# A gated mix of a state-space layer and linear attention on one Trainium2 core: the last fold of K's weight moved ahead of the vectors' transposes, eight idle products removed, the first two x tiles swapped, the last two rows scaled in halves

## The chip, the core and the metric

The kernel runs on one core of a Trainium2 chip. The metric is the time of one execution in device microseconds. The engines are named as in the profile: PE is TensorE (PEld its weight loads), DVE is VectorE, ACT is ScalarE, POOL is GpSimd, and SP is SyncE, which here only issues transfers. Each engine works through its own list of instructions in order and waits on semaphores of the others.

## What is computed

The input x has 2048 rows of 512 columns. Two branches take it, and a gate mixes them row by row.

```python
g = sigmoid((x * gate_w).sum(-1, keepdims=True))
# A: a diagonal complex recurrence
Lam_bar = exp(exp(log_dt) * Lam);  B_bar = ((Lam_bar - 1) / Lam)[:, None] * Bmat
h_t = Lam_bar * h_{t-1} + B_bar @ x_t
a = 2 * (hseq @ Cmat.T).real + x * Dskip
# B: linear attention, 32 heads of 16
q, k, v = split(x @ wqkv)
phi(u) = concat(softmax(u @ w_phi), softmax(-(u @ w_phi)))
kv = phi(k)^T v;  z = sum phi(k);  o = phi(q) kv / (phi(q) z + 1e-6)
out = g * a + (1 - g) * (o @ wo)
```

All inputs and the output are bfloat16.

## The kernel before, in words

The work is cut into stages, and each stage is a Python generator that yields after every few instructions. A string, `ORDER`, names a stage per word, and the loop at L804 takes one step of that stage for each word. So the string is the order in which instructions are issued, for all engines together; each engine gets its own instructions in that order. After a word, `@` gives the PSUM banks that the step takes, `:D` sends a copy out of PSUM to VectorE instead of ScalarE, `:A` sends a store to ScalarE's queue instead of SyncE's, and `F:n` issues n idle products (L810 to L812) of a constant tile into a bank that nothing reads. The loads of the first x tiles, of the weight of V (`Wv`) and of the small vectors stand ahead of that loop: SyncE issues the transposing loads of x tiles 0 to 3, then `Wv`, then tiles 4 to 7.

The words that the change and the prediction's steps touch:

- `W0` to `W3` (`st_W`, L271): TensorE transposes one block of K's weight, and a copy brings it back.
- `f0` to `f3` (`st_f`, `fold`, L428): four products of 128 columns multiply a block of K's weight by `w_phi`, and a copy writes the block of the folded weight `Wk2`.
- `V` (`st_V`, L308): TensorE transposes the three small vectors of the recurrence, VectorE copies them. `P`, `P2`, `P3`, `P4` and `U` compute the recurrence's angles and sizes from them, `i0` to `i3` tables of sines.
- `k0` to `k15` and `v0` to `v15` (L477, L484): four products of 512 columns for one tile of 128 rows of x, and one copy out of the bank. A product `k` needs its x tile and the four blocks of `Wk2` in turn.
- `l8` to `l15`: the loads of the later x tiles on SyncE.
- `o12` to `o15` (`st_o`, L725): the attention output of one tile of rows. For these four, TensorE transposes the result (L753) and the second-to-last step copies it out of PSUM (L755) into `oT`.
- `t0` to `t15` (`st_t`, L761): first step, four products of `oT` with `Wo` into the bank `py`; second step, the bank scaled by the gate `G` into the tile `ot`; third step, the store to the output. Row tiles are numbered in the order in which they are worked on, so t14 and t15 are the last two of 16.

The string ends, before and after the change, with these words:

```
t10:D t11 o15@2 o15 t10 o13:D t11 t11:A y13 t13 o14
o14@1 t15 t15 t15 o14:D t14 t13 t13 t14 t14:A
```

That is: row 14's transposes, then t15's products, t15's scaling, t15's store, the copy of row 14's `oT` on VectorE, t14's products, the scaling and store of t13, the scaling and store of t14.

Of the kernel before, what the change touches and what calls it, by code (L numbers as in the profile page):

```python
# [10 lines left out]
ALU = mybir.AluOpType  # L11
# [9 lines left out]
P = 128  # L21
MAGIC = 12582912.0
Z_MAX = 70.0
ORDER = """
NR F:28 NI B W1@0 W0@1 W0 W2@2 W1:D W3@3 W3 f1@4 W2:D f0@5 f2@6 f0 f1:D l10 V@0 F:4 V P f3@1 f3 f2:D F:4 P P k1@2 k1
l13 P2 k0@3 P2 U P2 P2 P2 P2 P4 k2@4 P3 P3 k3@5 P4 P4 k0 v0@0 i0 i2 U i0 i0 i1 i2 k4@7 i0:D i0 k2 i2 i2:D i2 U k3 k5@6
i1 v3@1 n0 x0 l9 i1 V2@2 i3 l12 x0 k4 v2@3 i3 i3 l14 i1 k5 n0 x0 n0 x0 i3 k7@4 n0 x0 U n0 i1 l11 k6@5 n1 x1 x1 n1 x1
n1 l8 R0 R1 x1 i3 k7 M v7@7 x1 n1 n1 k6:D L V2 v1@6 x2 n2 e0 v6@4 v5@5 v4@2 e0 x2 s0 v0 l15 n2 s0 n2 v2 s0 v1 R2 s0 v6
v3 n2 k10@0 k10 s0 k9@3 k9 C4 k13@6 gw D R3 s0 k12@4 e1 v7 s0 e1 s1 C6 k11@1 k11 x2 s1 k14@0 k8@3 k12 k14 k8 v4 k13
a0@71 a0 x2 s1 x2 s1 v5 g00@4 g00 g60@0 n2 x3 s1 g20@3 g60 s1 g10@2 g10 n3 e2 g30@6 g40@5 g10 s1 a1 x3 g20 n3 a1 x3 n3  # L30
x3 g41@4 n3 C3 e2 e2 e2 x3 g30 g40 g30 k15@0 k15 n3 e3 s2 x4 s2 x4 g01@2 g01 e3 e3 s2 g50@3 g11@5 g50 s2 s2 s2 n4 x4
n4 Q3 n4 s2 g50 g21@6 e3 s3 v8@0 g31@2 g11 Q2 g11 n4 g70@3 Q1 s3 C7 g21 g70 v9@5 g70 g70 z0 z0 g31 g31 Q0 w1@6 C0 a2
a2 a2 w0@3 s3 z0 v11@2 v9 g61@5 g41 R4 z0 w1 v8 z0 z0 g61 s3 w2@4 s3 s3 a2 x4 z0 z0 g51@6 g51 x4 w2 C2 s3 w3@0 g51 v11
n4 R5 w3 g71@5 g71 g71 g71 z1 z1 g02@4 g02 g42@6 a3 a3 z0 z0 g42 w0 e4 e4 z1 z1 z1 g62@2 g12@0 q1@5 C1 h50@4 C5 J1 e4
e4 z1 q2@6 q2 g12 g12 g22@3 g22 J0 h50 z1 z1 g62 q3@4 q3 J2 s4 z1 s4 q0@6 z1 s4 q0 q1 xA nA g32@0 J3 g32 g32 h60@3 J0
g52@2 g52 c4 h60 J2 c4 g52 h51@4 c2 s4 s4 g72@6 R7 g72 xA h10@5 nA g72 g72 c2 xA J3 nA h10 v10@0 v10 J1 s4 c5 h51 c5
R6 g23@3 v12@2 c4 c0 c0 g63@5 nA z2 z2 a3 a3 g03@4 xA g03 z2 z2 z2 z2 xA g23 z2 z2 g33@6 c5 v12 z2 z2 g13@0 g13 g63
g43@4 h32@3 g13 nA g43 h52@2 h52 g33 h32 h61@5 h61 h12@0 c0 g53@4 h12 g33 g53 s4 v14@3 c2 eA eA h42@2 h42 g73@6 g53 eA
# [30 lines left out]
def kernel(  # L69
# [18 lines left out]
    nc = tc.nc  # L88
    _, S, D = A_x.shape
# [5 lines left out]
    NTI = S // P  # L95
    NR = 8
# [7 lines left out]
    x2 = A_x[0]  # L104
# [3 lines left out]
    VS = nc.vector.tensor_scalar  # L108
# [3 lines left out]
    sel = {"banks": [], "eng": "act"}  # L112
# [66 lines left out]
    G = const.tile([P, NTI], F32, name="G")  # L179
# [581 lines left out]
    def st_t(n):  # L761
        ti = order[n]
        py, oT = live["py", n], live["oT", n]
        for g in range(HG):
            MM(out=py[:], lhsT=oT[:, g, :], rhs=Wo[:, g, :], start=False, stop=(g == HG - 1))  # L765
        yield
        ot = pools["op"][1].tile([P, D], BF16, name="ot", bufs=14)
        if sel["eng"] == "act":
            nc.scalar.mul(out=ot[:], in_=py[:], mul=G[:, ti:ti + 1])  # L769
        else:  # L770
            VS(out=ot[:], in0=py[:], scalar1=G[:, ti:ti + 1], scalar2=None, op0=ALU.mult)
        yield
        sel["q"].dma_start(out=out_par[:, ti // 2, ti % 2, :], in_=ot[:])
        yield
# [17 lines left out]
    for n in range(NTI):  # L792
        st.update({f"k{n}": st_k(n), f"v{n}": st_v(n), f"q{n}": st_q(n), f"y{n}": st_y(n), f"o{n}": st_o(n), f"t{n}": st_t(n)})
# [10 lines left out]
    for tok in ORDER.split():  # L804
        tok, _, eng = tok.partition(":")
# [42 lines left out]
```

## Time and profile before

| what | value |
|---|---|
| median of 3 runs | 155.96 us (155.78, 155.96, 157.13) |
| the profiled execution | 155.28 us |
| its span, first to last instruction | 153.2 us, mean granted TensorE clock 0.995 |
| TensorE busy | 146.2 us (95% of the span) |
| VectorE busy | 132.4 us (86%) |
| ScalarE busy | 129.2 us (84%) |
| transfers | 17.55 MB, 115 GB/s on the mean |

How to read the lines below. A row of the timeline gives the start (us from the span's start), the duration in us from the first start to the last end, engine, line, operation, output <- input, shapes and the number of merged instructions; a bracket at the end gives the idle time of that engine just before, and what ended it. Products are pipelined: one of 512 columns is shown with 0.38 us, while the next follows 0.22 us later. A row of the groups by shape ends with busy us, mean ns of one, idle us before them and what ended it. In the chain of waits each piece stands with its start, its duration and what it was. A row of the windows gives the stretch, its length, the busy time and count of each engine, then the granted TensorE clock (1.00 is full), the busy share of the DMA engines and GB/s. A few records of products are missing from the trace.

### The profile page before, as it was taken

The numbers are of one execution on the slowest core, as the hardware profiler recorded it, in microseconds if no ns is written. First come the engines' busy times: TensorE is split into PE (matmuls) and PEld (weight loads), VectorE is DVE, ScalarE is ACT, GpSimd is POOL, SyncE is SP. The second block draws the span as 40 slices with busy tenths as digits, with TensorE's granted clock in tenths as the row PEclk, the third lists the DMA queues.
The fourth block names the chain that finished last, engine by engine and source line by source line (L and its number), as shares of the span: only waits on it lengthen the run. The fifth ranks groups of instructions, "written<-read, shape, count | busy, mean of one in ns | idle before, by whom it ended". The sixth has DMA issues, their size and how long they took to land.

```text
span 153.2 us, 3361 instructions
## 1 busy us (share of the span) xinstructions
PE 146.2 (95%) x1236; PEld 95.0 (62%) x1254; DVE 132.4 (86%) x303; ACT 129.2 (84%) x279; POOL 15.8 (10%) x43
## 2 busy tenths in 40 slices
PE   7899999999999999999999999999999999999990
PEld 7644434788878985869867656555554455555540
DVE  3799999999999999999999999999999958717520
ACT  3489998999998999999998999699498998627562
POOL 8239980000000000000000000000000000000000
PEclk9999999999999999999999999999999999999997
DMA  4875995534445699930000007711278859969842
GB/s 116 164 218 97 223 178 112 103 75 103 103 107 78 129 230 178 166 115 4 0 0 4 0 0 169 74 37 34 42 98 147 176 122 189 162 129 206 247 143 103
DMA packets 50848, 17.55 MB, mean 115 GB/s; under 512 B 44176, under 2 KB 50832, under 8 KB 50832
## 3 DMA queue, kind: packets, MB, share of 16 engines
q1 hardware_dynamic: 48976, 15.75, 53.8%
q10 hardware_dynamic: 1696, 1.57, 3.2%
q8 instruction: 10, 0.16, 0.5%
q0 software_dynamic: 160, 0.01, 0.2%
q14 instruction: 6, 0.05, 0.1%
HBM read 2.64 MB, written 2.10 MB: 31 GB/s over the span
## 4 chain that ended last, share of the span: by engine, by line
PE 78%; SPq 10%; DMA 7%; issue 1%; ACT 1%
PE pgq L601 18%; PE py L717 16%; PE pq L475 9%; PE py L765 8%; SPq L229 8%; PE pv L475 4%; PE ph L668 4%; PE pk L475 4%; DMA xT<-in_A_x_dram 4%; PE kvacc L578 3%; DMA phT<-EEq 3%; PE pn L736 3%; PE pgq L606 2%; PE py L722 2%; PE pgq L608 2%; SPq L284 1%
## 5 line engine op out<-in xcount | busy, mean ns | idle before, releaser
L601 PE MATMUL pgq<-xT,BT 128*128 128x256 bf16 x256 | 31.5, 272 | 0.0
L475 PEld LDWEIGHTS <-xT 128*128 128x128 bf16 x192 | 18.2, 98 | 18.3 <-DMA xT<-in_A_x_dram 0.7
L601 PEld LDWEIGHTS <-BT 128*128 128x128 bf16 x256 | 24.6, 98 | 4.1
L138 ACT ACTIVATE EEk<-EEk 128x1024 bf16<-128x1024 bf16 x20 | 20.4, 1080 | 0.0
L119 ACT CAST uv<-pgq 128x512 bf16<-128x512 f32 x28 | 15.9, 605 | 0.5 <-PE pgq L601 0.4
L475 PE MATMUL pv<-Wv,xT 128*128 128x512 bf16 x59 | 15.5, 379 | 0.3
L475 PE MATMUL pq<-Wq,xT 128*128 128x512 bf16 x60 | 15.4, 379 | 0.2
L765 PE MATMUL py<-Wo,oT 128*128 128x512 bf16 x62 | 15.3, 379 | 0.1
L475 PE MATMUL pk<-Wk,xT 128*128 128x512 bf16 x62 | 14.7, 379 | 0.3 <-DMA xT<-in_A_x_dram 0.2
L138 ACT ACTIVATE EEq<-EEq 128x1024 bf16<-128x1024 bf16 x12 | 11.7, 1042 | 0.3 <-DVE EEq L527 0.3
L769 ACT ACTIVATE ot<-py,G 128x512 bf16<-128x512 f32 x12 | 7.9, 686 | 4.5 <-PE py L765 4.3
L138 ACT ACTIVATE ld<-pn 128x16 f32<-128x16 f32 x32 | 6.1, 191 | 5.7 <-PE pn L736 4.6
L590 ACT ACTIVATE phT<-X,dgB 128x512 bf16<-128x512 bf16 x16 | 10.7, 725 | 0.0
L119 ACT CAST nu<-pn 128x256 bf16<-128x256 f32 x27 | 9.9, 380 | 0.0
L119 ACT CAST vx<-pv 128x512 bf16<-128x512 f32 x16 | 9.1, 604 | 0.4 <-PE pv L475 0.4
L548 DVE TENSOR_TENSOR EEk<-EEk,rck 128x4096 bf16<-128x4096 bf16 (+1 forms) x5 | 9.3, 1858 | 0.0
L744 DVE TENSOR_TENSOR on<-nu,rd 128x512 bf16<-128x512 bf16 x16 | 6.7, 421 | 2.8 <-ACT rd L138 1.6
L765 PEld LDWEIGHTS <-oT 128*128 128x128 bf16 x64 | 5.7, 97 | 5.3 <-DMA oT<-on 0.5
L119 ACT CAST Xq<-pq 128x512 bf16<-128x512 f32 x16 | 8.9, 608 | 0.0
L119 ACT CAST Xq<-pk 128x512 bf16<-128x512 f32 x15 | 8.6, 598 | 0.4 <-PE pk L475 0.4
L736 PEld LDWEIGHTS <-phT 128*128 128x128 bf16 x128 | 6.2, 97 | 3.8 <-DMA phT<-EEq 1.4
L511 DVE TENSOR_TENSOR smk<-smk 128x512 bf16<-128x512 bf16 (+4 forms) x18 | 8.1, 448 | 0.1
(178 smaller groups left out, 321.2 us busy)
## 6 DMA issues: line engine op xcount, KB each, us to landing
X<-HM SPq DMA_DIRECT2D x8, 256.0 KB, 4.5
out_dram<-ot ACTq DMA_DIRECT2D x8, 128.0 KB, 2.5
out_dram<-ot SPq DMA_DIRECT2D x8, 128.0 KB, 2.2
C2r<-in_B_wqkv_dram ACTq DMA_DIRECT2D x2, 256.0 KB, 3.8
Wv<-in_B_wqkv_dram SPq DMA_DIRECT2D x1, 512.0 KB, 4.0
Bn<-in_A_B_re_dram SPq DMA_DIRECT2D x1, 512.0 KB, 5.7
Bn<-in_A_B_im_dram SPq DMA_DIRECT2D x1, 512.0 KB, 6.8
Wo<-in_B_wo_dram SPq DMA_DIRECT2D x1, 512.0 KB, 4.3
```

The lines of the kernel that those rows point to most:

```text
L119: nc.scalar.copy(out=out_ap, in_=in_ap)
L138: ins = nc.scalar.activation(**kw)
L229: nc.sync.dma_start_transpose(out=xT[:, :, ti * P:(ti + 1) * P], in_=x_res[ti // 2, ti % 2])
L475: MM(out=pt[:], lhsT=xT[:, kt, ti * P:(ti + 1) * P], rhs=W[:, kt, :], start=(kt == 0), stop=(kt == KT - 1))
L511: VT(out=dst, in0=cur[:, :, :, 0:n, :], in1=cur[:, :, :, n:2 * n, :], op=op)
L548: VT(out=E5, in0=E5, in1=rc.to_broadcast([P, L, 2 * NB, Dh, 4]), op=ALU.mult)
L590: nc.scalar.mul(out=t_, in_=x_, mul=c_)
L601: MM(out=pg[:, h, :], lhsT=BT[:, kt, 2 * j + h, :], rhs=xT[:, kt, r * NC:(r + 1) * NC], start=(h == 0 and kt == 0), stop=(r % 2 == 0 and k ...
L717: MM(out=py[:], lhsT=hs(r, t, slice(a * P, (a + 1) * P)), rhs=C2B[t], start=(t == 0), stop=False)
L736: MM(out=pn[:, 4 * m:4 * m + 4, :].rearrange("p h e -> p (h e)"), lhsT=ph[:, 4 * hf + m, :], rhs=KVm[:, 4 * hf + m, :], start=(m == 0), st ...
L765: MM(out=py[:], lhsT=oT[:, g, :], rhs=Wo[:, g, :], start=False, stop=(g == HG - 1))
L769: nc.scalar.mul(out=ot[:], in_=py[:], mul=G[:, ti:ti + 1])
```

## The change

It has two parts. In the front of the string:

```diff
-NR F:28 NI B W1@0 W0@1 W0 W2@2 W1:D W3@3 W3 f1@4 W2:D f0@5 f2@6 f0 f1:D l10 V@0 F:4 V P f3@1 f3 f2:D F:4 P P k1@2 k1
-l13 P2 k0@3 P2 U P2 P2 P2 P2 P4 k2@4 P3 P3 k3@5 P4 P4 k0 v0@0 i0 i2 ...
+NR F:28 NI B W1@0 W0@1 W0 W2@2 W1:D W3@3 W3 f1@4 W2:D f0@5 f2@6 f0 f1:D l10 f2:D f3@1 f3 V@0 V P P P k0@2 k0 l13 P2
+k1@3 P2 U P2 P2 P2 P2 P4 k2@4 P3 P3 k3@5 P4 P4 k1 v0@0 i0 i2 ...
```

All words behind `v0@0` are the same in the same order; the other lines of the string are only broken at other places. The copy of f2 (on VectorE), f3's products and f3's copy (on ScalarE) now stand ahead of `V`, the two groups `F:4` are gone (the 28 idle products at the start stay), and `k0` and `k1` change places, with the banks staying where they were.

In the last step of the output:

```diff
         ot = pools["op"][1].tile([P, D], BF16, name="ot", bufs=14)
-        if sel["eng"] == "act":
+        if n >= NTI - 2:
+            nc.scalar.mul(out=ot[:, 0:D // 2], in_=py[:, 0:D // 2], mul=G[:, ti:ti + 1])
+            VS(out=ot[:, D // 2:D], in0=py[:, D // 2:D], scalar1=G[:, ti:ti + 1], scalar2=None, op0=ALU.mult)
+        elif sel["eng"] == "act":
             nc.scalar.mul(out=ot[:], in_=py[:], mul=G[:, ti:ti + 1])
         else:
             VS(out=ot[:], in0=py[:], scalar1=G[:, ti:ti + 1], scalar2=None, op0=ALU.mult)
```

`NTI` is 16, so this holds for t14 and t15. Before, ScalarE scaled all 512 columns of both; now ScalarE scales the left 256 and VectorE the right 256, at the same place in the string. Each row's store is still one transfer of 512 columns.

More of the change, by code (lines that the diff above doesn't have):

```diff
@@ L24 @@
 ORDER = """
-NR F:28 NI B W1@0 W0@1 W0 W2@2 W1:D W3@3 W3 f1@4 W2:D f0@5 f2@6 f0 f1:D l10 V@0 F:4 V P f3@1 f3 f2:D F:4 P P k1@2 k1
[L26 to L34, printed above, removed]
@@ L35 @@
-e4 z1 q2@6 q2 g12 g12 g22@3 g22 J0 h50 z1 z1 g62 q3@4 q3 J2 s4 z1 s4 q0@6 z1 s4 q0 q1 xA nA g32@0 J3 g32 g32 h60@3 J0
+NR F:28 NI B W1@0 W0@1 W0 W2@2 W1:D W3@3 W3 f1@4 W2:D f0@5 f2@6 f0 f1:D l10 f2:D f3@1 f3 V@0 V P P P k0@2 k0 l13 P2
+k1@3 P2 U P2 P2 P2 P2 P4 k2@4 P3 P3 k3@5 P4 P4 k1 v0@0 i0 i2 U i0 i0 i1 i2 k4@7 i0:D i0 k2 i2 i2:D i2 U k3 k5@6 i1
+v3@1 n0 x0 l9 i1 V2@2 i3 l12 x0 k4 v2@3 i3 i3 l14 i1 k5 n0 x0 n0 x0 i3 k7@4 n0 x0 U n0 i1 l11 k6@5 n1 x1 x1 n1 x1 n1
+l8 R0 R1 x1 i3 k7 M v7@7 x1 n1 n1 k6:D L V2 v1@6 x2 n2 e0 v6@4 v5@5 v4@2 e0 x2 s0 v0 l15 n2 s0 n2 v2 s0 v1 R2 s0 v6 v3
@@ new lines @@
+n2 k10@0 k10 s0 k9@3 k9 C4 k13@6 gw D R3 s0 k12@4 e1 v7 s0 e1 s1 C6 k11@1 k11 x2 s1 k14@0 k8@3 k12 k14 k8 v4 k13 a0@71
+a0 x2 s1 x2 s1 v5 g00@4 g00 g60@0 n2 x3 s1 g20@3 g60 s1 g10@2 g10 n3 e2 g30@6 g40@5 g10 s1 a1 x3 g20 n3 a1 x3 n3 x3
+g41@4 n3 C3 e2 e2 e2 x3 g30 g40 g30 k15@0 k15 n3 e3 s2 x4 s2 x4 g01@2 g01 e3 e3 s2 g50@3 g11@5 g50 s2 s2 s2 n4 x4 n4
+Q3 n4 s2 g50 g21@6 e3 s3 v8@0 g31@2 g11 Q2 g11 n4 g70@3 Q1 s3 C7 g21 g70 v9@5 g70 g70 z0 z0 g31 g31 Q0 w1@6 C0 a2 a2
+a2 w0@3 s3 z0 v11@2 v9 g61@5 g41 R4 z0 w1 v8 z0 z0 g61 s3 w2@4 s3 s3 a2 x4 z0 z0 g51@6 g51 x4 w2 C2 s3 w3@0 g51 v11 n4
@@ L36 @@
+R5 w3 g71@5 g71 g71 g71 z1 z1 g02@4 g02 g42@6 a3 a3 z0 z0 g42 w0 e4 e4 z1 z1 z1 g62@2 g12@0 q1@5 C1 h50@4 C5 J1 e4 e4
+z1 q2@6 q2 g12 g12 g22@3 g22 J0 h50 z1 z1 g62 q3@4 q3 J2 s4 z1 s4 q0@6 z1 s4 q0 q1 xA nA g32@0 J3 g32 g32 h60@3 J0
 g52@2 g52 c4 h60 J2 c4 g52 h51@4 c2 s4 s4 g72@6 R7 g72 xA h10@5 nA g72 g72 c2 xA J3 nA h10 v10@0 v10 J1 s4 c5 h51 c5
```

## The prediction

> **What bounds the kernel now.** I read the chain of waits on the page, then the same chain in order of time, then the timeline around the two places that the change touches.
>
> ```profile
> PE 78%; SPq 10%; DMA 7%; issue 1%; ACT 1%
> ```
>
> ```profile
> 17.02 5.82 DMA xT<-in_A_x_dram
> ...
> 22.89 5.35 PE pk L475 x24
> ```
>
> TensorE carries 78% of the chain, but not from the beginning: until 22.84 us it runs through SyncE's list of loads and an x tile that was issued at 17.02 and took 5.82 us. What TensorE does before 22.89 isn't on it. Now the front itself, in the timeline:
>
> ```profile
> 5.64 0.97 PE L431 MATMUL pf<-BD,Xq 128*128 128x128 bf16 x12
> ...
> 6.90 0.16 PE L310 MATMUL pvt<-ident,vec_n 12*128 12x12 bf16 x1 [0.29 <-DMA vec_n<-in_A_log_dt_dram]
> 6.99 0.40 PE L812 MATMUL spin<-fillw 128*128 128x128 bf16 x4
> ...
> 7.22 0.39 PE L431 MATMUL pf<-BD,Xq 128*128 128x128 bf16 x4
> ...
> 7.45 0.39 PE L812 MATMUL spin<-fillw 128*128 128x128 bf16 x4
> ...
> 7.67 3.62 PE L475 MATMUL pk<-Wk,xT 128*128 128x512 bf16 x15
> ...
> 11.12 1.03 PE L475 MATMUL pv<-Wv,xT 128*128 128x512 bf16 x4
> ```
>
> ```profile
> 22.88 4.86 PEld L475 LDWEIGHTS <-xT 128*128 128x128 bf16 x24 [0.65 <-DMA xT<-in_A_x_dram]
> ```
>
> Three folds end at 6.61, TensorE stands until the vectors land (6.90), then come four idle products, the last fold, four more, and K's products from 7.67. At 22.88 the weight load has been idle 0.65 us for that x tile: TensorE is already early there.
>
> The tail, timeline and the output tile's last transfer:
>
> ```profile
> 147.28 1.89 PE L765 MATMUL py<-Wo,oT 128*128 128x512 bf16 x8
> ...
> 147.48 0.42 DVE L121 COPY oT<-po 128x512 bf16<-128x512 bf16 x1 [1.06 <-PE po L753]
> 148.34 1.84 ACT L769 ACTIVATE ot<-py,G 128x512 bf16<-128x512 f32 x3 [1.00 <-PE py L765]
> 149.06 0.91 SPq L773 DMA_DIRECT2D out_dram<-ot  x2
> 150.22 0.34 ACTq L773 DMA_DIRECT2D out_dram<-ot  x1
> ```
>
> ```profile
> 148.79 0.38 PE L765 MATMUL py<-Wo,oT 128*128 128x512 bf16 x1
> ```
>
> ```profile
> 149.50 0.69 ACT L769 ACTIVATE ot<-py,G 128x512 bf16<-128x512 f32 x1
> ```
>
> ```profile
> DMA to landing us min/median/max: 2.0/2.0/2.0
> ```
>
> Eight products follow each other: t15's four, then t14's four, whose last ends at 149.17. ScalarE scales t15, t13, t14 in that order, t14 at 149.50 because it is third in the queue. Its store is issued at 150.22 and lands 2.0 us later, which ends the kernel (span 153.2). Note the VectorE copy at 147.48: it fetches row 14's transposed tile, which t14's products need, and it runs while TensorE is at t15.
>
> **The front, part by part.** First group to fold, fold to second group, second group to K take 0.23, 0.23 and 0.22 us: the eight idle products are worth 0.45, the fold 0.23. The fold goes into the gap between 6.61 and 6.90. Then the evacuations decide:
>
> ```profile
> 6.06 0.69 DVE L121 CAST Wk<-pf 128x512 bf16<-128x512 f32 x1
> 6.42 0.58 ACT L119 CAST Wk<-pf 128x512 bf16<-128x512 f32 x1
> ...
> 7.10 0.17 DVE L312 CAST vec<-pvt 128x12 f32<-128x12 bf16 x1 [0.34 <-PE pvt L310]
> ...
> 7.18 0.68 DVE L121 CAST Wk<-pf 128x512 bf16<-128x512 f32 x1
> ...
> 7.30 0.21 ACT L138 ACTIVATE ssm_par<-vec 128x4 f32<-128x4 f32 x1 [0.29 <-DVE vec L312]
> ...
> 7.65 0.59 ACT L119 CAST Wk<-pf 128x512 bf16<-128x512 f32 x1
> ...
> 7.78 0.16 DVE L337 TENSOR_TENSOR ssm_par<-vec,ssm_par 128x8 f32<-128x8 f32 x1
> ```
>
> K's first product needs f0's copy, done at 7.00, so it can start at about 7.05, 0.62 earlier. VectorE's second copy moves up from 7.18 to about 6.68 and ends at 7.36; ScalarE's second from 7.65 to 6.92, ending 7.50. K's 16 products take 11.12 - 7.67 = 3.45, 0.216 each, so the third and fourth start at 7.48 and 7.70, after these copies. The vectors' copy now queues behind VectorE's: 7.30 to 7.47, exponential 7.50 to 7.71, the product at 7.78 where it stood before. So the sines' chain on VectorE neither gains nor loses. Tile 0 first, tile 1 second:
>
> ```profile
> L229 SPq DMA_TRANSPOSE xT<-in_A_x_dram x1: 1275/1275/1275, 1.3 to 1.3; - x1
> ...
> DMA to landing us min/median/max: 4.5/4.5/4.5
> ```
>
> ```profile
> L229 SPq DMA_TRANSPOSE xT<-in_A_x_dram x1: 1254/1254/1254, 2.6 to 2.6; - x1
> ...
> DMA to landing us min/median/max: 4.7/4.7/4.7
> ```
>
> Tile 0 is there at 5.8, tile 1 at 7.3; at 7.05 tile 1 would have been late, so the swap is what lets the early start happen. It costs nothing else, since the pair of evacuations keeps its places.
>
> ```profile
> 6.57 0.58 SPq L238 DMA_DIRECT2D Wv<-in_B_wqkv_dram  x1
> ```
>
> ```profile
> Wv<-in_B_wqkv_dram SPq DMA_DIRECT2D x1, 512.0 KB, 4.0
> ```
>
> V's first product would start at 7.05 + 3.45 = 10.50, but Wv lands at 10.57: the lead shrinks to about 0.5 us. SyncE's instructions are the same in the same order as built, and none of its early loads waits for an engine, so the x tile that TensorE waits for at 22.88 still lands at 22.84. The lead of 0.5 becomes a wait of 0.5 there. Price of the front: 0. From below, if that tile didn't bind, -0.5; from above nothing, as nothing on the chain starts later.
>
> **The tail.** Prices, from the groups by shape:
>
> ```profile
> L119 ACT CAST uv<-pgq 128x512 bf16<-128x512 f32 x28 | 15.9, 605 | 0.5 <-PE pgq L601 0.4
> ...
> L119 ACT CAST nu<-pn 128x256 bf16<-128x256 f32 x27 | 9.9, 380 | 0.0
> ```
>
> ```profile
> L771 DVE TENSOR_SCALAR ot<-py,G 128x512 bf16<-128x512 f32 x4 | 3.0, 750 | 4.2 <-PE py L765 4.1
> ...
> L121 DVE CAST nu<-pn 128x256 bf16<-128x256 f32 x5 | 2.0, 423 | 2.6 <-ACT ld L138 2.6
> ```
>
> Halving the columns saves ScalarE 605 - 380 = 0.225, so its half scaling costs 0.69 - 0.225 = 0.465. On VectorE 0.68 (the 512-column copy above) against 0.423 saves 0.26, so 0.75 - 0.26 = 0.49. Bounds: 0.38 and 0.42 (a plain copy) below, 0.69 and 0.75 (no saving) above. I take the middle ones, since the same pairs of shapes give them.
>
> Do the halves run side by side? Both read one PSUM bank. Where the kernel now has two readers of one bank (the logarithm and the copy of one `pn`):
>
> ```profile
> 138.01 0.20 ACT L138 ACTIVATE ld<-pn 128x16 f32<-128x16 f32 x1
> ...
> 138.24 0.42 DVE L121 CAST nu<-pn 128x256 bf16<-128x256 f32 x1 [1.89 <-ACT ld L138]
> ```
>
> VectorE starts 0.03 after ScalarE has finished. As built, VectorE's half waits for ScalarE's semaphore likewise, at the count of its own row's half: first ScalarE, then VectorE, 0.465 + 0.035 + 0.49 = 0.99 against 0.69 whole. [...]
>
> Worse is what queues behind. In program order row 15's scaling comes before row 14's copy (`t15` stands before `o14:D`). Scaling used to be ScalarE's; now VectorE's list as built ends: half of t15, copy of row 14's tile, half of t14. The copy, so far at 147.48, must wait for t15's last product. Step by step:
>
> - t15's products end 148.31 (ScalarE starts at 148.34 now). ScalarE half 148.34 to 148.81.
> - VectorE half 148.84 to 149.33.
> - Copy from 149.25 (VectorE overlaps by 0.08: 7.78 against 7.18 + 0.68) to 149.67.
> - t14's four products from 149.72: three steps of 0.216 and 0.38 make 150.75. They started at 148.14 before.
> - ScalarE half 150.78 to 151.25, VectorE half 151.28 to 151.77, store issued at 151.80 instead of 150.22.
>
> So +1.6 us. t13's scaling (from 148.72) and SyncE's two stores (149.4 and 149.8, behind t15's half) are done long before. The store lands 2.0 later as now. Lowest prices: 2 x (0.085 + 0.07) = 0.3 less, +1.3; highest: 2 x (0.225 + 0.26) = 1.0 more, +2.6.
>
> **Sum.** Front 0, tail +1.6. The profiled execution took 155.28 (span 153.2 and 2.1 around it), so 156.9 against it. The median of the runs shown, 155.96, is 0.7 above; against it 157.5.
>
> **Rivals.**
>
> 1. The front's gain is kept: in place of a wait at 22.88 TensorE runs on. For it: TensorE is solid from there to 116.7. Against it: the 0.65 idle there, on a tile whose issue doesn't move. Price -0.5: 157.0, or 156.4 on the profile's base. It decides from the tile landing 0.4 us earlier on.
> 2. TensorE's clock falls in the new gap, 148.36 to 149.72:
>
> ```profile
> 148.00:151.60 3.60, 1.17 (x6) 0.35 (x4) 0.00 (x0) 1.84 (x3) 0.00 (x0) 1.00 0.43 149
> 151.70:153.20 1.50, 0.00 (x0) 0.00 (x0) 0.00 (x0) 0.00 (x0) 0.00 (x0) 0.50 0.00 0
> ```
>
>    It was granted fully until 2.4 us or more after the last product and then halved. The new gap is 1.4 us. At half clock t14's four products cost 4 x 0.216 = 0.86 more: +2.5, 158.4. [...] Highest prices of the halves end at the same place, +2.6.
> 3. The other side, not slower: VectorE isn't held, so that row 14's copy leaves at 147.48 as now. Then t14's products end at 149.17, its halves run 149.31 (behind t13's scaling) to 149.77 and 149.81 to 150.30, store at 150.33: +0.1, 156.1. It decides from the copy starting ahead of t15's half. Against it: VectorE's built list, and no row of the trace has it run out of order.
> 4. Halves truly side by side, the copy still held: t15's half to 148.83, copy to 149.17, products to 150.25, t14's halves to 150.74, store 150.78: +0.56, 156.5. Against it: the 0.03 row and the built wait.
>
> **Chances.** Forecast 72%, front kept in part or whole 13%, clock or full price 9%, side by side 3%, copy not held 3%. One per cent, about what can be told from no change, is 1.56 us: the forecast's +1.6 lies on that line. Of its 72, 41 lie above it, with the 9 of rival 2 that makes slower 50%; the rest of it and rivals 1, 3, 4 make 48% within 1%. No case is faster by 1%; 2% for what I don't see. Range: from 156.4 (rivals 1 and 4) to 158.5 (rival 2).
>
> **What would show it.** Right: K's first product near 7.05, the wait at 22.88 grown to about 1.1 us of idle weight load, TensorE from there on as before to 148.3; VectorE's copy of row 14 near 149.25, t14's products near 149.72, the last store near 151.8. The front is wrong if the products at 22.89 start earlier; the tail is wrong if the copy stays near 147.5 or a VectorE half starts with its ScalarE half.

## The result, and the profile after

| | before | after |
|---|---|---|
| median | 155.44 us (20 runs, 154.82 to 157.23) | 157.57 us (20 runs, 156.81 to 158.87) |
| ratio, 95% interval | | 1.0131 [1.0105, 1.0156] |
| profiled execution, its span | 155.28 us, 153.2 | 157.09 us, 155.1 |
| mean granted TensorE clock | 0.995 | 0.998 |

The change makes the kernel slower by 1.3%: 2.0 us of 155.4, between 1.6 and 2.4. The forecast was 157.5 and +1.6 us. That the time was met so closely is luck: the 155.96 that the sum was set on lies 0.5 above the median that this kernel shows with more runs, the change cost 0.4 more than predicted, and the two errors cancel. The ratios, here and below, leave out slow executions and are not the quotients of the medians beside them, so the two can differ by some tenths of a us.

The front in the profile of after, timeline. In this execution the first loads landed 0.3 to 0.5 us earlier than in that of before, so the order and the idle times count, not the absolute starts.

```profile
5.37 1.24 PE L431 MATMUL pf<-BD,Xq 128*128 128x128 bf16 x16
...
6.54 0.18 PE L310 MATMUL pvt<-ident,vec_n 12*128 12x12 bf16 x1
...
6.69 3.62 PE L475 MATMUL pk<-Wk,xT 128*128 128x512 bf16 x15
...
7.43 0.17 DVE L337 TENSOR_TENSOR ssm_par<-vec,ssm_par 128x8 f32<-128x8 f32 x1 [0.27 <-ACT ssm_par L138]
```

The weight loads a little later, with their idle time and what ended it:

```profile
10.56 1.41 PEld L475 LDWEIGHTS <-xT 128*128 128x128 bf16 x8 [0.74 <-DMA Wv<-in_B_wqkv_dram]
```

The four folds are one group of 16, the vectors' transpose follows without a gap, and K's products start at 6.69 instead of 7.67. Then `Wv` stops TensorE, as predicted: the weight load idles 0.74 us. The same engine at the x tile that bound before:

```profile
22.38 4.86 PEld L475 LDWEIGHTS <-xT 128*128 128x128 bf16 x24 [0.48 <-DMA xT<-in_A_x_dram]
```

It stopped TensorE again. The idle did not grow to the 1.1 us of the forecast, since here another 0.34 stands one group of four products earlier (at 21.36), and the tile itself landed 0.5 earlier.

The tail in the timeline:

```profile
147.71 1.03 PE L765 MATMUL py<-Wo,oT 128*128 128x512 bf16 x4
...
148.77 0.47 ACT L769 ACTIVATE ot<-py,G 128x256 bf16<-128x256 f32 x1 [1.00 <-PE py L765]
149.14 0.68 ACT L772 ACTIVATE ot<-py,G 128x512 bf16<-128x512 f32 x1
149.28 0.48 DVE L770 TENSOR_SCALAR ot<-py,G 128x256 bf16<-128x256 f32 x1 [2.64 <-ACT ot L769]
149.68 0.42 DVE L121 COPY oT<-po 128x512 bf16<-128x512 bf16 x1
...
150.15 1.04 PE L765 MATMUL py<-Wo,oT 128*128 128x512 bf16 x4 [1.42 <-DVE oT L121]
151.23 0.47 ACT L769 ACTIVATE ot<-py,G 128x256 bf16<-128x256 f32 x1 [1.40 <-PE py L765]
151.73 0.48 DVE L770 TENSOR_SCALAR ot<-py,G 128x256 bf16<-128x256 f32 x1 [1.64 <-ACT ot L769]
152.25 0.34 ACTq L776 DMA_DIRECT2D out_dram<-ot  x1
```

And the chain of waits there, in order of time (start, duration, what):

```profile
148.77 0.48 ACT ot L769
149.25 0.02 issue
149.28 0.48 DVE ot L770
149.76 0.34 DVE oT L121
150.11 0.05 issue
150.15 1.05 PE py L765 x4
```

VectorE stands idle for 2.64 us until ScalarE's half of t15 is done, and only then copies row 14's tile (149.68, once 147.48). TensorE waits 1.42 us for that copy, in the middle of what were eight products without a gap. From the start of t15's scaling to the last store, before took 150.22 - 148.34 = 1.88 us and after takes 152.25 - 148.77 = 3.48: **+1.60, the sum predicted as +1.6**. But t15's scaling itself starts 0.43 later than before (148.77 against 148.34), though K's products had started earlier. Something in between cost time. The waits of the weight loads in after name one place:

```profile
PEld L765 <- DVE oT L121: 1.9, 1, 1.9
PEld L765 <- DMA oT<-on: 1.3, 2, 1.1
```

The columns are the wait in total, how often, and the longest. In before the second row reads:

```profile
PEld L765 <- DMA oT<-on: 0.5, 2, 0.3
```

A transposing load of `oT`, which no part of the change touches, now stops TensorE's weight loads for 1.1 us. An earlier place is a weight load of `phT`, in the timeline of before and then of after:

```profile
117.45 0.30 PEld L736 LDWEIGHTS <-phT 128*128 128x128 bf16 x8 [0.34 <-DMA phT<-EEq]
```

```profile
117.53 0.31 PEld L736 LDWEIGHTS <-phT 128*128 128x128 bf16 x8 [0.77 <-DMA phT<-EEq]
```

TensorE had been 0.56 us ahead of before at `Wv` and 0.36 through the middle. Behind this load it is 0.08 late. But two groups of `phT` further on it gets that back, since there it is before that waits longer. Again before, then after:

```profile
121.13 0.31 PEld L736 LDWEIGHTS <-phT 128*128 128x128 bf16 x8 [0.67 <-DMA phT<-EEq]
```

```profile
120.75 0.40 PEld L736 LDWEIGHTS <-phT 128*128 128x128 bf16 x8 [0.22 <-DMA phT<-EEq]
```

Behind these, after is 0.28 ahead again. It loses its lead at `oT`, in before and in after:

```profile
135.23 0.69 PEld L765 LDWEIGHTS <-oT 128*128 128x128 bf16 x4 [0.17 <-DMA oT<-on]
```

```profile
135.88 0.55 PEld L765 LDWEIGHTS <-oT 128*128 128x128 bf16 x4 [1.09 <-DMA oT<-on]
```

From there to the end it is 0.4 to 0.5 late. So in this profile the 0.4 beyond the tail are lost at the loads of `oT`, not at those of `phT`.

### The profile page after: what moved, and what is told of

It reads as the page before. It is cut to its first block, busy times and chain, and to the rows that moved or that the text cites. A ratio compares the mean times of both kernels' runs of the same rounds, so it can differ in the third digit from the quotient of the medians.

```text
span 155.1 us, 3346 instructions
## 1 busy us (share of the span) xinstructions
PE 146.4 (94%) x1228; PEld 94.5 (61%) x1246; DVE 133.3 (86%) x305; ACT 129.1 (83%) x279; POOL 13.3 (9%) x43
## 3 DMA queue, kind: packets, MB, share of 16 engines
HBM read 2.64 MB, written 2.10 MB: 31 GB/s over the span
## 4 chain that ended last, share of the span: by engine, by line
DVE 57%; PE 16%; ACT 12%; DMA 8%; issue 3%; ACTq 1%; DVEq 0%; SPq 0%
PE py L717 8%; DVE smk L511 7%; PE py L765 5%; DVE mnk L511 4%; ACT EEk L138 4%; DVE mxk L511 3%; DVE EEk L548 3%; DVE HM L672 3%; DMA oT<-on 3%; DMA phT<-EEq 3%; DVE Bn L672 3%; DVE w L641 3%; DVE H L652 3%; DVE EEk L527 2%; DVE EEk L521 2%
## 5 line engine op out<-in xcount | busy, mean ns | idle before, releaser
L772 ACT ACTIVATE ot<-py,G 128x512 bf16<-128x512 f32 x10 | 6.8, 686 | 4.0 <-PE py L765 3.9
```

## The experiments

Two theories went in: either the halves' held copy explains the whole loss and the front is worth nothing, or the front has a price of its own. Each ratio is against runs of before on the same chip.

**The front alone.** ORDER as changed, all rows scaled whole:

```diff
-        if n >= NTI - 2:
-            nc.scalar.mul(out=ot[:, 0:D // 2], ...
-            VS(out=ot[:, D // 2:D], ...
-        elif sel["eng"] == "act":
+        if sel["eng"] == "act":
```

> Only the new front of the string; the last rows are scaled whole as before. Theory (the front's lead is taken back by the wait for an x tile near 22 us, the loss is all in the tail): 0.0 us against before, within 0.3, with K's first product near 7.0 and the products of the x tile that lands near 22.5 starting when it lands. Rival A (the front itself costs something further on, and is the 0.4 us by which the change lost more than the tail's 1.6): +0.4. Rival B (the front's lead is kept): -0.5, and then the tail would have cost 2.5.

Measured: 156.26 against 155.59, 1.0035 [1.0003, 1.0067], +0.55 us. The front isn't free.

**The halves alone.** The old string with the halves of the change's diff.

> Only the halves of the last two rows; the string as before. Theory: +1.6 us against before, with row 14's copy on VectorE about 0.9 us behind the start of row 15's scaling. Rival A (front costs 0.4): also +1.6, and the changed kernel's measured +2.0 then is the sum. Rival B (front gains 0.5): +2.5.

Measured: 156.83 against 155.59, 1.0082 [1.0050, 1.0114], +1.3 us (0.8 to 1.8). Its profile has 3.47 us from t15's scaling to the last store, against 1.88. Front and halves add up: 0.35% + 0.82% = 1.17%, beside the 1.31% of both.

**The copy ahead of t15's halves.** The whole change, with VectorE's list no longer holding the copy:

```diff
-o14@1 t15 t15 t15 o14:D t14 t13 t13 t14 t14:A
+o14@1 t15 o14:D t15 t15 t14 t13 t13 t14 t14:A
```

> The changed kernel with one word moved: row 14's copy stands ahead of row 15's scaling, so that VectorE makes the copy before the half that waits for ScalarE. Theory (most of the loss is the held copy, not the halves): +0.1 us against before, the copy near 147.5 to 147.9 and t14's products directly behind t15's. Rival C (the two halves one behind the other are the loss themselves, whatever VectorE does between): it stays at +1.0 to +1.6. With rival A, 0.4 more than the theory says.

Measured: 156.63 against 155.59, 1.0071 [1.0042, 1.0101], +1.1 us. By its time alone rival C (+1.0 to +1.6) could stand, as what is left is more than the front's +0.55. But the stretch from t15's scaling to the last store is back at 1.96 us, and the interval's lower end, +0.65, is the front's price and the halves' 0.1 together. The run with both mended, below, decides it.

**t13 scaled ahead of t15.** Before, with only the tail's words changed:

```diff
-o14@1 t15 t15 t15 o14:D t14 t13 t13 t14 t14:A
+o14@1 t15 t13 t13 t15 t15 o14:D t14 t14 t14:A
```

> The kernel before with one pair of words moved: t13 is scaled and stored ahead of t15's scaling, all on ScalarE and in whole rows. Theory (before, t14's scaling was late only because it stood third in ScalarE's queue, 0.33 us behind its last product): t14's scaling starts 0.03 behind its last product, the last store leaves 0.3 us earlier, -0.3 us against before. Rival D (the end is set by the stores' landing, not by when the last is issued): 0.0.

Measured: 155.16 against 155.59, 0.9973 [0.9951, 0.9995], -0.4 us. The timeline of its tail:

```profile
147.47 1.27 ACT L769 ACTIVATE ot<-py,G 128x512 bf16<-128x512 f32 x2 [0.42 <-PE po L753]
...
148.92 0.69 ACT L769 ACTIVATE ot<-py,G 128x512 bf16<-128x512 f32 x1 [0.18 <-PE py L765]
149.64 0.34 ACTq L773 DMA_DIRECT2D out_dram<-ot  x1
```

ScalarE is idle 0.18 us ahead of t14, where before it came late to it because t13 stood in between. From the start of t15's products to the last store it now takes 149.64 - 146.99 = 2.65 us against 150.22 - 147.28 = 2.94: the 0.3 that was expected, by order alone, without any halves.

**The idle products alone.** After the front's +0.55, the next question was which part of it costs. Theory F of the expectations below says that the shorter list of TensorE moves the fetches of its code, and that these hold up other transfers; rival G says that this is worth nothing. Before, with nothing but both `F:4` taken out of the string:

```diff
-... f0 f1:D l10 V@0 F:4 V P f3@1 f3 f2:D F:4 P P k1@2 k1
+... f0 f1:D l10 V@0 V P f3@1 f3 f2:D P P k1@2 k1
```

> The kernel before with only the two groups of four idle products near 7 us taken out, nothing reordered. Theory F: as the new front alone, +0.55 us, with the fetch near 115.3 and the third transpose near 115.5 taking the long issue. Rival G: 0.0.

Measured: 156.28 against 155.71, 1.0037 [1.0009, 1.0065], +0.6 us (0.1 to 1.0): as much as the front alone loses, with no fold and no tile moved. Removing eight products that nothing reads makes the kernel slower.

**Eight idle products elsewhere.** The front alone, with the same number of products put back where TensorE waits for the x tile anyway (called the padding below):

```diff
-n2 k10@0 k10 s0 k9@3 k9 ...
+n2 k10@0 k10 s0 F@3:8 k9@3 k9 ...
...
+            pad = bank([P, 512], F32, "pad") if banks else spin
...
-                MM(out=spin[:, 0:P], ...
+                MM(out=pad[:, 0:P], ...
```

> The new front with whole rows at the end, and eight idle products put in front of the products that wait for an x tile near 22.4 us, so that TensorE's list has its old length again from there on. Theory F (the 0.55 us that the front alone costs comes from TensorE's instruction fetches: with 16 instructions fewer each 16 KB fetch moves about 1.2 us and meets other transposing loads, near 113 to 117 and 130 to 136 us): the fetches are back at about 114.0 and 132.4, the second of the four transposes near 114 takes the long issue again, and the time is that of before, 0.0 us within 0.3. Rival G (the reordering of evacuations and tiles in the front costs it): +0.55 stays.

Measured: 155.59 against 155.71, 0.9999 [0.9973, 1.0024]. The loss is gone, as theory F had it. (The front alone ran on another chip, the kernel without the idle products on this one.)

**The padding on before.** To see whether such products gain time by themselves:

> The kernel before with eight idle products added at the same x tile's wait: TensorE's list is 16 instructions longer, all else as it was. Theory F: the fetches come about 1.2 us earlier, near 112.8 and 131.2, and other transposes take the long issue; the time changes although the products stand in a wait, by +-0.2 to 0.8 us, which sign the theory can't say ahead. Rival G: 0.0 (0.1 us of products beyond the wait at most).

Measured: 156.15 against 155.71, 1.0014 [0.9984, 1.0043]. They gain nothing; whether they cost a little can't be told.

What connects these runs is a row of the DMA queues that the prediction didn't look at. The page of before has it:

```profile
q8 instruction: 10, 0.16, 0.5%
```

That is ten transfers of 16 KB of code within the kernel (packets, MB, share of 16 engines' span). In before TensorE begins about 253 products and weight loads on the mean between one fetch and the next (from 223 to 311), in after about 253 too (from 234 to 289), so I take the fetches to follow TensorE's list. One of them falls among SyncE's transposing loads of `phT`. Below are those loads (timeline of SyncE in narrow windows: start, time to issue) for before, for the kernel without the idle products and for the front with padding, each followed by the row of the DMA view that shows the fetch in a window of 0.2 us. Before, with the fetch between 113.9 and 114.1:

```profile
113.03 1.25 SPq L563 DMA_TRANSPOSE phT<-EEq  x1
...
114.37 2.25 SPq L563 DMA_TRANSPOSE phT<-EEq  x1
```

```profile
q8 instruction: 1, 0.02, 47.5%
```

Without the idle products, the fetch between 115.6 and 115.8, and then the piece of the chain of waits that starts at the first load:

```profile
113.10 1.24 SPq L563 DMA_TRANSPOSE phT<-EEq  x1
...
115.82 2.23 SPq L563 DMA_TRANSPOSE phT<-EEq  x1
```

```profile
q8 instruction: 1, 0.02, 39.7%
```

```profile
113.10 4.80 DMA phT<-EEq
```

Front with padding, between 113.8 and 114.0:

```profile
112.92 1.24 SPq L563 DMA_TRANSPOSE phT<-EEq  x1
...
114.25 2.25 SPq L563 DMA_TRANSPOSE phT<-EEq  x1
```

```profile
q8 instruction: 1, 0.02, 47.3%
```

In these three the load issued within 0.4 us behind the fetch's start takes 2.2 us to issue instead of 1.25. With the long list of TensorE that is the second load; with eight products (16 instructions with their weight loads) fewer, the fetch comes 1.7 us later and hits the third. The first load, on which TensorE waits, then lands after 4.8 us instead of 4.4. So does after: its fetch shows between 115.2 and 115.4, and its loads are issued at 112.67, 114.01 and 115.40, the third in 2.22 us. The list's length is not all, though: with eight products more than before has, the fetch was expected near 112.8, but came at 114.03, and the first load took the long issue (113.57, 2.02 us).

For the time this place matters little. With the second load held up, the third is issued later, and TensorE waits there instead. Set beside before, weight load by weight load, the five kernels with the short list lose 0.3 to 0.5 us at the first of these loads, and all but 0.1 of it is back at the third.

A second place comes near 133, with the three transposing loads of `oT`. The DMA view from 130 to 137 us gives the share of another code queue, q14, and these loads' median us to landing, for four kernels in turn. Before:

```profile
q14 instruction: 1, 0.01, 0.5%
...
oT<-on SPq DMA_TRANSPOSE x3, 3.8
```

After:

```profile
q14 instruction: 1, 0.01, 1.3%
...
oT<-on SPq DMA_TRANSPOSE x3, 4.4
```

Without the idle products:

```profile
q14 instruction: 1, 0.01, 1.6%
...
oT<-on SPq DMA_TRANSPOSE x3, 4.9
```

The front with padding:

```profile
q14 instruction: 1, 0.01, 0.5%
...
oT<-on SPq DMA_TRANSPOSE x3, 4.1
```

Where this fetch takes three times as long, the `oT` tiles land late and TensorE stands. Its start and length part all 14 profiles of the study: in seven the fetch started at 132.78 us or earlier and took at most 0.65 us, and the loads came in time; in seven it started at 132.88 or later, took at least 1.46 us, and they came late. Which of the two delays the other, and whose code it is, these traces don't tell.

Here the time is lost: against before, the seven late profiles lose 0.7 to 1.5 us at these loads, the others at most 0.4. And the seven go with the list's length, but not strictly. All five kernels with the short list are among them (the change twice, the front alone, the copy ahead, and no idle products), and so is before with eight products more; of the eight with the length of before, seven are in time and one is late. One profile of each kernel can't tell in what share of its executions the loads come late.

**Copy ahead, and padding.** If both causes are found, the change with both mended should be back at before, but for the halves themselves:

> The changed kernel with row 14's copy ahead of row 15's scaling and the eight idle products at the x tile's wait: the new front and the serial halves stay, the held copy and the moved fetches go. If the change's loss is the held copy (1.5) plus the moved fetches (0.55) and the halves one behind the other cost 0.1: +0.1 us against before. If the serial halves cost more than the trace shows: +0.5 or more, as the 1.1 of the copy-ahead run less the fetches' 0.55.

Measured: 155.58 against 155.52, 1.0009 [0.9979, 1.0038]. So halves that hold nobody cost about 0.1 us, and rival 3's size was right for the case in which VectorE isn't held. Its timeline:

```profile
147.42 0.42 DVE L121 COPY oT<-po 128x512 bf16<-128x512 bf16 x1 [0.82 <-PE po L753]
148.28 0.47 ACT L769 ACTIVATE ot<-py,G 128x256 bf16<-128x256 f32 x1 [1.00 <-PE py L765]
...
149.73 0.48 DVE L770 TENSOR_SCALAR ot<-py,G 128x256 bf16<-128x256 f32 x1 [0.46 <-ACT ot L769]
150.25 0.34 ACTq L776 DMA_DIRECT2D out_dram<-ot  x1
```

**The change and padding.** The whole change with the padding alone, twice, and the change itself on the second chip:

> The changed kernel with the eight idle products at the x tile's wait and nothing else: the fetches are back, the tail stays as changed. If losses add: +1.3 to +1.6 us against before, that is 0.55 better than the change. If the tail hides or doubles the fetches' loss: +2.0, or under 1.0.

> The changed kernel with the eight idle products at the x tile's wait once more, beside the changed kernel itself on the same chip. The first run gave +2.0 us from six executions, and its profile showed the late transposes near 135 us although the products were there. If these late transposes come in a share of the executions that the length of TensorE's list only shifts: now between +1.3 and +2.0, and 0.2 to 0.7 below the changed kernel beside it, with executions of both kinds. If the padding does nothing once the tail is changed: the same time as the changed kernel, within 0.2.

> The changed kernel itself on the same chip, as the partner: +2.0 us against before, within 0.4.

Measured: 1.0131 [1.0080, 1.0182] (157.79 against 155.52) and 1.0118 [1.0071, 1.0164] (157.10 against 155.49); the change itself 1.0161 [1.0119, 1.0204] (157.78 against 155.49). In both padded profiles the fetch near 114 is back where before has it (114.25 and 113.98, against 115.36 for the change itself). In one of them, though, the `oT` loads were late again (q14's fetch at 133.52, 1.84 us). Side by side the padding gives 0.68 us back in the median, but the intervals overlap: with the halves in, this is inconclusive. The first padded run even met the rival's +2.0, not the +1.3 to +1.6 of losses that add.

**The front with padding and t13 early**, both kernels' better parts in whole rows:

> The new front, the eight idle products at the x tile's wait, and t13 scaled ahead of t15 in whole rows. Theory F: the early t13's gain alone, -0.3 to -0.45 us against before, and nothing from the front. Rival G: +0.1 to +0.25.

Measured: 155.39 against 155.71, 0.9964 [0.9939, 0.9988], -0.56 us. It beats both kernels. The tail's order alone had given -0.4, and the front with padding nothing, so its gain is that of the order.

## Why the prediction was right, and which step of it failed

**The held copy: right, and its size too.** +1.6 predicted, +1.60 in the profile, +1.3 [0.8, 1.8] for the halves alone. Step by step from t15's ScalarE half: VectorE's half +0.50 predicted and +0.51 measured, copy +0.91 and +0.91, t14's products +1.38 and +1.38, its ScalarE half +2.44 and +2.46, store +3.46 and +3.48. The halves took 0.47 and 0.48 us against 0.465 and 0.49.

**Halves one after the other: right.** VectorE's half starts at 149.28, ScalarE's ended at 149.24. Rival 4 (side by side) falls: it wanted the store 2.44 us after t15's scaling, 3.48 was measured. As written, the kernel orders the two by a semaphore; what two unordered readers would do was not tried.

**The clock: right to be a rival, and refuted.** TensorE's granted clock stayed full through the 1.4 us gap (1.00 from 148.7 to 150.2). The prediction's own rows show the clock of before full until 151.60 and halved from 151.70 on, about 2.5 us after the last product's end at 149.17. In after it stood at 1.00 from 151.20 to 154.50 and at 0.50 from 154.60 on, about 3.4 us after the last product's end at 151.19. The gap of 1.4 us was shorter than either. The page of after shows the clock slice by slice (a 9 is 90% or more):

```profile
PEclk9999999999999999999999999999999999999999
```

**VectorE not held (rival 3): refuted for the change**, and shown to be the cure by the two runs with the copy ahead.

**The front's gain is swallowed: right.** `Wv` took back what lay above 0.56 us of lead, the front alone was slower than before, and with padding level with it. Rival 1 (-0.5 us) falls. By the prediction's own sign the front would look wrong, since the products that started at 22.89 in before start at 22.38 in after; but the tile landed as much earlier, and TensorE still stood for it. Such landings vary: in the nine profiles with the new front TensorE is, at 60 us, between 0.36 us ahead of before's profile and 0.53 behind it.

**The front's price: wrong.** The step read "Price of the front: 0 ... from above nothing, as nothing on the chain starts later". It measured +0.55 us (0.05 to 1.0). The chain was followed only to 22.88, with the argument that SyncE's instructions are the same in the same order. They are, but what they meet is not the same: with 16 instructions fewer on TensorE the fetch near 114 comes 1.3 to 1.8 us later, and in every profile with so short a list the loads of `oT` near 133 came late. The prediction's bound from above should have held a term for transfers that change neighbours. The chain and the timelines it read don't show them; the table of DMA queues names the fetches. None of its rivals was this case: its chances add up to 100 without it, and the 2% "for what I don't see" stand beside them.

How far this is shown: that taking out the eight idle products alone brings the loss, and that the front with eight such products elsewhere is level with before, is measured. That the fetch near 114 moves, and with it the slow load, stands in the traces, but TensorE gets its delay back. In the profiles the time is lost at the `oT` loads, and more of it (0.8 to 1.5 us with the short list) than the medians differ by. Why these loads come late stays open, and so does whether the moved fetches are the reason. Also open: the padding uses up the lead as well as restoring the list's length (in that profile it runs from 22.46, and K's next product comes at 23.12), and the two were not tried apart.

## What to carry to other kernels

When part of an operation moves to another engine, ask first what stands behind it in that engine's list: the halves themselves cost about 0.1 us, the copy queued behind one of them 1.5. Before splitting a row between two engines that read one bank in turn (0.99 us against 0.69 whole), look for another order of whole rows, which here gave 0.4 us. And if a change that only removes instructions makes a kernel slower, put as many harmless ones back at another place before believing a story about the ones removed.

## What the runs showed of the hardware

Code was fetched while the kernel ran, over the DMA queues: ten transfers of 16 KB here (q8 instruction, 0.16 MB), for 1228 products and 1246 weight loads of TensorE as the page of after counts them. Between one of these fetches and the next TensorE began about 253 products and weight loads on the mean, in before as in after. With 16 instructions fewer in the list, one fetch came 1.7 us later (115.7 us against 114.0). In the profiles of before, of after, of the kernel without the idle products and of the front with padding, the transposing load of `phT` issued within 0.4 us behind this fetch's start took 2.2 us to issue instead of 1.25. With the fetch at the third load instead of the second, the first landed after 4.8 us instead of 4.4; TensorE had that back at the third.
